# Attention and MLP on one Trainium2 core: other slots for the background weight conversion, GpSimd's operand split a slot later, v asked for sooner, one result of the mixing pairs later

## The chip, the core and the metric

The kernel runs on one core of a Trainium2 chip. The metric is the device time of one execution in microseconds. The engines in what follows are TensorE (PE, with its weight loads as PEld), VectorE (DVE), ScalarE (ACT), GpSimd (POOL) and SyncE (SP), which here does nothing but issue DMAs, in program order.

## The reference, cut to what matters

```python
scores = scale * np.matmul(q, k.transpose(0, 1, 3, 2))      # 4 batches, 8 heads, 576 x 576, head size 64
...
scores = scores + bias.transpose(2, 0, 1)[None, :, :, :]    # bias from a small net on log distances
attn = np.exp(scores - max) / (sum + 1e-09)
x = (attn @ v) laid out as 4 x 576 x 512
h = x.transpose(0, 2, 1) @ U @ V                             # mixing along the sequence, rank 32
u = x + h.transpose(0, 2, 1)
out = u + np.maximum(u @ w_ch1, 0.0) @ w_ch2                 # 512 -> 2048 -> 512
```

U, V, w_ch1 and w_ch2 arrive as 64-bit floats, seen as pairs of 32-bit words. The kernel turns them into 32-bit floats on the chip; that is the conversion the change is about.

## The kernel before

**Pairs and slots.** Two heads of one batch make a pair; there are 16 (p = 0 to 15, four to a batch). A pair has nine slots (s = 0 to 8), and `slot(p, s)` writes the instructions of one slot for all engines; each engine then runs its own list in that order. In a slot TensorE computes one block of scores (`sc`, L319). VectorE adds the bias and takes the row extreme (`p` or `praw`, L321), which is also what frees the scores' PSUM bank (two banks). ScalarE takes the exponential (L340). TensorE transposes earlier blocks (`tb`, `tm`, `ti`, L387 to L407), ScalarE or VectorE copy them to `pt`, and two runs of 20 matmuls multiply with v (`o`, L423): half 0 of a pair at the end of its slot 8, half 1 in slot 3 of the next pair. `assemble(p - 1, 0)` and `assemble(p - 1, 1)`, in slots 4 and 8, transpose that product (`tx`) and write it, scaled, to `x_sb` on VectorE (L446, L369). The transposes and `tx` share three PSUM banks in turn.

**The split.** Matmuls take q and k as a high part (`hi`) and a remainder (`lo`). GpSimd makes them for the next pair in four steps, `prep_ops`: high of q (L151), remainder of q (L159, two instructions), high of k (L151), remainder of k (L159, two), one step per slot from slot 2 on. They read `raw`, a single buffer that SP refills in two parts in slots 5 and 7 for the pair after next. `v` of the next pair is asked for in slot 7 and has two buffers. GpSimd also scales a block called `pm` in slot 1 (L360, two instructions).

**The conversion.** `conv_ops` gives the seven operations of one job of 128 x 256 values: a load of `wraw` (SP); size and low (ScalarE, L187 and L190); clamp, shift and join (VectorE, L193, L199, L205); add (GpSimd, L210). Twenty jobs run behind attention: one for U, three for V, sixteen for the first quarter of the weights. `pipeline` chops a job into the groups [size, low], [clamp, shift], [join, add]; `background(1)` issues one group after each slot in `conv_at` from `CONV_FROM` on. Once it is running, the odd job has its groups in slots 7, 8 and 0 and the even one in slots 1, 2 and 6.

**Mixing pairs.** After a batch is complete, pairs 5, 9 and 13 also run the mixing: `mix_t` in slot 0, then `mix_h` for rows 4, 0, 1, 2, 3 in slots 1 to 5. Each `mix_h` has VectorE add into `x_sb` (L485) and SP write that block of `x_sb` to `u_dram` (L486). `assemble(p - 1, 0)` of such a pair overwrites blocks 0, 1 and 4 of `x_sb`, which those writes must have read by then.

**After attention** the MLP runs on TensorE (L569, L592), with further conversions behind it.

Of the kernel before, what the change touches and what calls it, by code (L numbers as in the profile page):

```python
# [19 lines left out]
HP = H // 2  # L20
# [8 lines left out]
K0 = 2 * S + LEFT  # L29
QKW = 2 * K0  # L30
# [7 lines left out]

AV_NEW, AV_OLD, AV_LAST = 8, 3, 2

CONV_FROM = (2, 0)
F64_LO = 2.0**-15
F64_HI = (1.875 - 2.0**-23) * 2.0**16

# [2 lines left out]
def kernel(  # L47
# [82 lines left out]
    def load_part(p, a, e):  # L130
        b, hp = divmod(p, HP)
        for lo in (0, D):
            nc.sync.dma_start(out=raw[lo : lo + D, a:e], in_=qk[b, hp, :, a:e])

    def load_v(p):
        b, hp = divmod(p, HP)
        v_t[p] = vpp.tile([P, 640], F32, tag="v", name="v")
        nc.sync.dma_start(out=v_t[p], in_=vp[b, hp])
# [36 lines left out]
    def conv_ops(src, n, finish):  # L175
        st = {}

        def load():
            st["raw"] = wrawp.tile([P, CW], I64, tag="wraw", name="wraw")
            nc.sync.dma_start(out=st["raw"][:, 0:n], in_=src)  # L180
            words = st["raw"].bitcast(I32).rearrange("p (n t) -> p n t", t=2)
            st["l"], st["h"] = words[:, 0:n, 0], words[:, 0:n, 1]

        def size():
            st["t"] = wcp.tile([P, CW], I32, tag="t", name="wt")[:, 0:n]
            st["y"] = wyp.tile([P, CW], I32, tag="wy", name="wy")[:, 0:n]
            nc.scalar.activation(out=st["t"].bitcast(F32), in_=st["h"].bitcast(F32), func=AF.Abs)  # L187

        def low():
            nc.scalar.activation(out=st["y"], in_=st["l"].bitcast(U32), func=AF.Copy, scale=2.0**-29)  # L190

        def clamp():
            nc.vector.tensor_scalar(  # L193
                out=st["t"].bitcast(F32), in0=st["t"].bitcast(F32),
                scalar1=F64_LO, scalar2=F64_HI, op0=ALU.max, op1=ALU.min,
            )

        def shift():
            nc.vector.tensor_scalar(  # L199
                out=st["t"], in0=st["t"], scalar1=3, scalar2=0x3FFFFFF8,  # L200
                op0=ALU.logical_shift_left, op1=ALU.bitwise_and,
            )

        def join():
            nc.vector.scalar_tensor_tensor(  # L205
                out=st["t"], in0=st["h"], scalar=sgn, in1=st["t"], op0=ALU.bitwise_and, op1=ALU.bitwise_or
            )

        def add():
            nc.gpsimd.tensor_tensor(out=st["y"], in0=st["t"], in1=st["y"], op=ALU.add)  # L210

        return load, [size, low, clamp, shift, join, add], lambda: finish(st["y"].bitcast(F32))
# [77 lines left out]
    def new_pair(p):  # L290
        st = stp.tile([P, 32], F32, tag="st", name="st")
        pair[p] = {"st": st, "P": {}}
# [87 lines left out]
    def tr(p, c, hd, eng):  # L380
        hf, o = q_off(c)
        pt = get_pt(p, hf)
        src = pair[p]["P"][c]
        bank = psum("t", [P, 4, P], "tb")
        b0 = 0 if hd == 0 else S + LEFT
        for kb in range(4):
            nc.tensor.transpose(bank[:, kb, :], src[:, b0 + kb * P : b0 + (kb + 1) * P], ident)  # L387
        copy(eng, pt[:, 5 * hd : 5 * hd + 4, o : o + P], bank)
# [99 lines left out]
    NP = B * HP  # L488

    def slot(p, s):  # L490

        new, old = p < NP, p > 0
        if new:
            scores(p, s)
        if old and s == (AV_OLD if new else AV_LAST):
            av(p - 1, 1)
        if old and s == 0:
            tr(p - 1, 3, 0, "a")
        elif old and s == 1:
            tr(p - 1, 3, 1, "a")  # L500
            tr_mid(p - 1, 1, "d")
        elif old and s == 4:
            assemble(p - 1, 0)
        elif old and s == 8:
            assemble(p - 1, 1)
        if new and 3 <= s <= 8:
            c, hd = divmod(s - 3, 2)
            tr(p, c, hd, "a" if p % HP == 1 and 2 < s < 6 else "da"[hd])
            if s == 5:
                tr_m(p, "a")  # L510
            elif s == 6:
                tr_mid(p, 0, "d")
        if new:
            exps(p, s)
        if s > 0 and new:
            recip(p, s - 1)
        elif s == 0 and old:
            recip(p - 1, 8)
        if new and s == AV_NEW:
            av(p, 0)  # L520
# [15 lines left out]
    def load_acc(i):  # L536
        nc.sync.dma_start(out=acc[i], in_=u_dram[i * P : (i + 1) * P, :])
# [76 lines left out]
    def fin_w(dst):  # L614
        return lambda y: nc.sync.dma_start(out=dst, in_=y)

    def pipeline(jobs):


        ops = [conv_ops(*j) for j in jobs]  # L620
        groups = [[ops[0][0], ops[1][0]]]
        end = None
        for i, (_, o, fin) in enumerate(ops):
            if i + 2 < len(ops):
                groups[-1].append(ops[i + 2][0])
            size, low, clamp, shift, join, add = o
            groups += [[size, low], [clamp, shift], [join, add]]
            if end is not None:
                groups[-2].append(end)
            end = fin  # L630
        return groups + [[], [end]]

    def weight_jobs(g, fin):
        jobs = []
        for which in range(2):
            for k in range(KD):
                for a in range(0, DM, CW):
                    if which == 0:
                        src = w_ch1[k * P : (k + 1) * P, g * DM + a : g * DM + a + CW]
                    else:  # L640
                        r = (g * FG + k) * P
                        src = w_ch2[r : r + P, a : a + CW]
                    jobs.append((src, CW, fin(g, which, k, a, a + CW)))
        return jobs

    queue = []
# [54 lines left out]
    jobs = [(u32, 160, fin_u)]  # L701
    jobs += [(v4[:, a : min(a + CW, 640)], min(CW, 640 - a), fin_v(a, min(a + CW, 640))) for a in range(0, 640, CW)]
    jobs += weight_jobs(0, lambda g, which, k, a, e: fin_w(wq_dram[4 * which + k, :, a:e]))
    queue += pipeline(jobs)
    queue[1:1] = [[]] * 3

    conv_at = (0, 1, 2, 6, 7, 8)

    def big_views(t, parts):

# [20 lines left out]
    for p in range(NP):  # L731
        if p > 0:
            new_pair(p)
        if 0 < p < HP - 1:
            bias[p + 1] = big.tile([P, 9 * S], F32, tag=f"big{p + 1}", name=f"bias{p + 1}")
            loads = [o for c in (4, 0, 1, 2, 3) for o in bias_loads(c, p + 1)]
        for s in range(9):
            if s == (1 if p else 0) and p < NP - 1:
                prep = prep_ops(p + 1)
            if s in ((2, 3, 4, 5) if p else (0, 1, 2, 3)) and p < NP - 1:  # L740
                prep.pop(0)()
            if s in (5, 7) and 0 < p < NP - 2:
                load_part(p + 2, *((0, K0) if s == 5 else (K0, QKW)))
            if s == 7 and 0 < p < NP - 1:
                load_v(p + 1)
            for o in loads[0:2]:
                o()
            del loads[0:2]
            if p > 0 or s not in early.values():
                if p > HP and p % HP == 1 and s == 0:  # L750
                    mix_t(p // HP - 1)
                slot(p, s)
                background(int(s in conv_at and (p, s) >= CONV_FROM))
            if p > HP and p % HP == 1:
                for c in {1: (4,), 2: (0,), 3: (1,), 4: (2,), 5: (3,)}.get(s, ()):
                    mix_h(p // HP - 1, c)
            if p == NP - 3 and s == 1:
                t = big.tile([P, 9 * S], F32R, tag="big0", name="w1q")
                *wq[0], uth[0] = big_views(t, [(WQ, KD), (WQ, KD), (LINE, None), (UT, KD)])
                feed = first_weights(0)  # L760
            if p == NP - 2 and s == 1:
                t = big.tile([P, 9 * S], F32R, tag="big1", name="w2q")
                w2a, w2b, utl[0] = big_views(t, [(WQ, KD), (WQ, KD), (LINE, None), (UT, KD)])
                wq[0] += [w2a, w2b]
                feed = first_weights(1)
            if p == NP - 1 and s == 1:
                t = big.tile([P, 9 * S], F32, tag="big2", name="acc")
                acc.update(enumerate(big_views(t, [(DM, 0)] * 10)))
                feed = iter(())
            if p >= NP - 3 and s in (1, 2, 4, 5, 7, 8):  # L770
                next(feed, None)
            if p == NP - 1 and s in (1, 2, 3, 4, 5):
                load_acc(2 * s - 2)
                load_acc(2 * s - 1)
            if p == NP - 1 and s in (6, 7):
                make_ut(0, s - 6)
# [64 lines left out]
    for n in range(2, NG * NB + 1):  # L841
        g, j = divmod(n, NB)
# [88 lines left out]
```

## Time and profile before

| what | value |
|---|---|
| median of 3 runs (lowest, highest) | 767.35 us (767.05, 771.42) |
| the profiled execution's own time | 770.71 us |
| its span in the profile | 768.9 us |
| PE, DVE, ACT, POOL busy | 739.8, 442.5, 358.4, 237.9 us |
| mean granted TensorE clock | 0.997 of full speed |

The profile is one execution. Busy time of TensorE is modelled and says little about how long it waits; the waits are read from the idle time noted on a row, and from the chain of work that ended last. Pairs are told apart by the start of the matmuls with v in slot 8: pair 10, for example, lies between 232.97 and 250.38 us, and its slot 0 begins when that run of matmuls of pair 9 ends.

### The profile page before, as it was taken

Reading aid. Unit: us, or ns where it says so; the run is one execution under the profiler, and the core shown is the slowest. Engines: PE = TensorE matmul, PEld = TensorE weight load, DVE = VectorE, ACT = ScalarE, POOL = GpSimd, SP = SyncE. Lnnn points to the kernel's source line nnn. Section 1 sums busy time; section 2 is a strip of 40 time slices with the busy share of each in tenths; the row PEclk is TensorE's granted clock in tenths of the full one; section 3 lists DMA queues with packets and bytes.
Section 4 is the critical chain, followed back from the end, with each engine's and each line's share of the span. In section 5 each row is a group of like instructions: output and inputs, shape, how many; then the busy total and the mean of one; then the engine's idle time right before and its main releaser. Section 6 shows DMA issues by size and latency. Waiting matters only on the chain.

```text
span 768.9 us, 14017 instructions
## 1 busy us (share of the span) xinstructions
PE 739.8 (96%) x5380; PEld 616.7 (80%) x5380; DVE 442.5 (58%) x942; ACT 358.4 (47%) x803; POOL 237.9 (31%) x252
## 2 busy tenths in 40 slices
PE   6989998999999998999999999999999999999998
PEld 4436786777777777878889889988999999899986
DVE  7995588788878875752448734662237722221222
ACT  7996776777767775873125513431124410111010
POOL 0004658646655556620015502540015500000000
PEclk9999999999999999999999999999999999999999
DMA  7798995464445444540153301320002200001111
GB/s 213 244 313 271 260 267 148 135 177 131 125 144 165 137 120 135 155 140 1 35 192 110 97 1 42 98 81 1 1 28 83 69 1 1 1 28 55 55 42 68
DMA packets 41618, 84.02 MB, mean 109 GB/s; under 512 B 7248, under 2 KB 9936, under 8 KB 41296
## 3 DMA queue, kind: packets, MB, share of 16 engines
q1 hardware_dynamic: 41552, 83.13, 36.4%
q8 instruction: 42, 0.69, 0.4%
q14 instruction: 24, 0.20, 0.1%
HBM read 60.96 MB, written 22.15 MB: 108 GB/s over the span
## 4 chain that ended last, share of the span: by engine, by line
PE 70%; DVE 10%; ACT 8%; DMA 5%; issue 3%; POOL 2%; SPq 1%; DVEq 0%; ACTq 0%; POOLq 0%
PE po L592 24%; PE ph L569 23%; PE o L423 7%; PE sc L319 6%; PE tb L387 4%; ACT ring L244 2%; DVE p L321 2%; ACT p L340 2%; DVE wt L199 2%; DVE wt L193 2%; ACT ring L266 2%; DMA bias_dram<-ring 1%; DMA v<-in_vp_dram 1%; DMA raw<-in_qk_dram 1%; DVE wt L205 1%
## 5 line engine op out<-in xcount | busy, mean ns | idle before, releaser
L574 ACT ACTIVATE hh<-ph 128x1024 fp32r<-128x1024 f32 x36 | 36.9, 1026 | 207.5 <-PE ph L569 207.5
L575 DVE SCALAR_TENSOR_TENSOR hh<-ph,hh 128x1024 fp32r<-128x1024 f32 x36 | 44.1, 1224 | 141.4 <-ACT hh L574 141.4
L210 POOL TENSOR_TENSOR wy<-wt,wy 128x256 int32<-128x256 int32 (+1 forms) x68 | 50.0, 735 | 239.3 <-DVE wt L205 215.5
L340 ACT ACTIVATE p<-p,st 128x576 f32<-128x576 f32 x128 | 99.8, 780 | 30.6 <-DVE st L321 30.6
L319 PE MATMUL sc<-hi 128*128 128x288 f32 x320 | 100.9, 332 | 2.7 <-DVE st L321 2.7
L592 PE MATMUL po<-wq,hh 128*128 128x512 f32 x432 | 103.2, 395 | 0.0
L321 DVE CUSTOM_DVE_ANT_0 p<-sc,bias 128x576 f32<-128x576 f32 x128 | 95.5, 749 | 12.4 <-PE sc L319 7.1
L592 PE MATMUL po<-w2q,hh 128*128 128x512 f32 x432 | 101.7, 391 | 0.9 <-DVE acc L595 0.9
L592 PEld LDWEIGHTS po<-wq,hh 128*128 128x128 f32 x432 | 80.1, 188 | 17.5
L569 PE MATMUL ph<-ut,w1q 128*128 128x256 f32 x768 | 94.2, 280 | 0.0
L592 PEld LDWEIGHTS po<-w2q,hh 128*128 128x128 f32 x432 | 79.9, 188 | 17.1 <-issue 1.1
L569 PEld LDWEIGHTS ph<-ut,w1q 128*128 128x128 f32 x768 | 92.1, 188 | 1.5 <-issue 0.6
L595 DVE TENSOR_TENSOR acc<-po,acc 128x512 f32<-128x512 f32 x72 | 49.5, 689 | 73.2 <-PE po L592 73.2
L569 PEld LDWEIGHTS ph<-ut,wq 128*128 128x128 f32 x768 | 90.3, 188 | 1.4
L569 PE MATMUL ph<-ut,wq 128*128 128x256 f32 x768 | 90.6, 277 | 0.0
L319 PE MATMUL sc<-lo,hi 128*128 128x288 f32 x320 | 89.7, 296 | 0.3 <-POOL lo L159 0.3
L423 PE MATMUL o<-pt,v 128*64 128x320 f32 (+1 forms) x640 | 85.4, 411 | 2.9 <-DMA v<-in_vp_dram 2.8
L387 PE MATMUL tb<-ident,p 128*128 128x128 f32 x512 | 78.8, 277 | 5.1 <-DVE x_sb L369 3.2
L319 PEld LDWEIGHTS sc<-hi 128*128 128x128 f32 x320 | 60.6, 189 | 15.4 <-issue 6.6
L387 PEld LDWEIGHTS tb<-ident,p 128*128 128x128 f32 x512 | 60.2, 141 | 14.4 <-ACT p L340 7.3
L423 PEld LDWEIGHTS o<-pt,v 128*64 128x64 f32 x640 | 44.4, 137 | 33.0 <-DMA v<-in_vp_dram 3.1
L367 ACT COPY pt<-tb 128x512 f32<-128x512 f32 x88 | 50.9, 578 | 27.6 <-PE tb L387 27.6
(92 smaller groups left out, 1044.0 us busy)
## 6 DMA issues: line engine op xcount, KB each, us to landing
raw<-in_qk_dram SPq DMA_DIRECT2D x56, 304.0 KB, 4.6
wraw<-in_w_ch_dram SPq DMA_DIRECT2D x64, 256.0 KB, 2.7
bias_dram<-ring SPq DMA_DIRECT2D x36, 288.0 KB, 4.3
v<-in_vp_dram SPq DMA_DIRECT2D x16, 320.0 KB, 5.4
bias<-bias_dram SPq DMA_DIRECT2D x16, 288.0 KB, 5.7
acc<-u_dram SPq DMA_DIRECT2D x18, 256.0 KB, 4.8
out_dram<-acc SPq DMA_DIRECT2D x18, 256.0 KB, 2.0
bias<-bias_dram SPq DMA_DIRECT2D x16, 256.0 KB, 5.5
```

Of the source, the lines that this page charges most:

```text
L210: nc.gpsimd.tensor_tensor(out=st["y"], in0=st["t"], in1=st["y"], op=ALU.add)
L319: mm(ps[:, a, 0:HALF], lhsT=hi[:, q0 : q0 + P], rhs=kk, start=(i == 0), stop=(i == n - 1))
L321: nc.vector.tensor_tensor_reduce(out=halves(dst), in0=ps[:, :, 0:HALF], in1=halves(bias[hp][:, s * S : (s + 1) * S]), scale=-0.125, scalar ...
L340: nc.scalar.activation(out=dst, in_=dst, func=AF.Exp, bias=st[:, s : s + 1], scale=-1.0, accum_out=st[:, 10 + s : 11 + s])
L367: nc.scalar.copy(out=out, in_=in_)
L387: nc.tensor.transpose(bank[:, kb, :], src[:, b0 + kb * P : b0 + (kb + 1) * P], ident)
L423: mm(o[hd * D : (hd + 1) * D, 0:n], lhsT=v[:, vb * D : (vb + 1) * D], rhs=pt[:, pb, :], start=(j == 0), stop=(j == 4),)
L569: mm(st["ps"][:, f, :], lhsT=w, rhs=u[:, k, :], start=(i == 0), stop=(i == 3 * KD - 1))
L574: nc.scalar.activation(out=hh[n], in_=st["ps"], func=AF.Relu)
L575: nc.vector.scalar_tensor_tensor(out=hl[n], in0=st["ps"], scalar=0.0, in1=hh[n].bitcast(F32), op0=ALU.max, op1=ALU.subtract)
L592: mm(ps, lhsT=h, rhs=w, start=(m == 0), stop=(m == 3 * FG - 1))
L595: nc.vector.tensor_tensor(out=a, in0=ps, in1=a, op=ALU.add)
```

## The change

`by_twos` takes the place of `pipeline` for the conversions behind attention. It takes two jobs a and b at a time and makes five groups: [size a, low a, a load, the end of the job before], [size b, low b], [clamp a, shift a], [join a, add a], [clamp b, shift b, join b, add b, the end of a, a load]. With `conv_at = (0, 2, 6, 7, 8)` and a start in slot 6 of pair 2 these fall in slots 6, 7, 8, 0 and 2; slot 1 carries none. The split's steps move from slots 2 to 5 to slots 3 to 6, the loads of `raw` from slots 5 and 7 to 6 and 8, and the load of v from slot 7 to slot 4. In mixing pairs `assemble(p - 1, 0)` moves from slot 4 to slot 6.

```diff
-CONV_FROM = (2, 0)
+CONV_FROM = (2, 6)
...
-        elif old and s == 4:
+        elif old and s == (6 if p > HP and p % HP == 1 else 4):
             assemble(p - 1, 0)
...
+    def by_twos(jobs):
+
+        ops = [conv_ops(*j) for j in jobs]
+        for load, _, _ in ops[:2]:
+            load()
+        groups, end = [], None
+        for i in range(0, len(ops), 2):
+            (_, a, end_a), (_, b, end_b) = ops[i : i + 2]
+            ahead = [load for load, _, _ in ops[i + 2 : i + 4]]
+            groups += [
+                a[0:2] + ahead[0:1] + ([end] if end else []), b[0:2], a[2:4], a[4:6], b[2:6] + [end_a] + ahead[1:2]
+            ]
+            end = end_b
+        return groups + [[end]]
...
-    queue += pipeline(jobs)
-    queue[1:1] = [[]] * 3
-
-    conv_at = (0, 1, 2, 6, 7, 8)
+    conv_at = (0, 2, 6, 7, 8)
...
-            if s in ((2, 3, 4, 5) if p else (0, 1, 2, 3)) and p < NP - 1:
+            if s in ((3, 4, 5, 6) if p else (0, 1, 2, 3)) and p < NP - 1:
                 prep.pop(0)()
-            if s in (5, 7) and 0 < p < NP - 2:
-                load_part(p + 2, *((0, K0) if s == 5 else (K0, QKW)))
-            if s == 7 and 0 < p < NP - 1:
+            if s == 4 and 0 < p < NP - 1:
                 load_v(p + 1)
+            if s in (6, 8) and 0 < p < NP - 2:
+                load_part(p + 2, *((0, K0) if s == 6 else (K0, QKW)))
+            if (p, s) == (CONV_FROM[0], 0):
+                queue += by_twos(jobs)
```

What the engines' lists look like at three places. First GpSimd over one plain pair with conversions (`pm` in slot 1, `hi` and `lo` the split, `wy` the add of a job). Before:

```order
L360 TENSOR_SCALAR pm<-praw,st 128x576
L360 TENSOR_SCALAR pm<-praw,st 128x64
L151 TENSOR_SCALAR hi<-raw 128x1216
L159 TENSOR_TENSOR hi<-raw,hi 64x608 x2
L151 TENSOR_SCALAR hi<-raw 128x1216
L159 TENSOR_TENSOR lo<-raw,hi 128x608 x2
L210 TENSOR_TENSOR wy<-wt,wy 128x256 x2
```

After, the same stretch:

```order
L360 TENSOR_SCALAR pm<-praw,st 128x576
L360 TENSOR_SCALAR pm<-praw,st 128x64
L210 TENSOR_TENSOR wy<-wt,wy 128x256
L151 TENSOR_SCALAR hi<-raw 128x1216
L159 TENSOR_TENSOR hi<-raw,hi 64x608 x2
L151 TENSOR_SCALAR hi<-raw 128x1216
L159 TENSOR_TENSOR lo<-raw,hi 128x608 x2
L210 TENSOR_TENSOR wy<-wt,wy 128x256
```

One of the two adds, which waits for VectorE's join of slot 2, now stands ahead of the whole split.

On VectorE, slots 2 and 3 of the same kind of pair (`p` the scores, `wt` the job's intermediate). Before:

```order
L352 RECIPROCAL st<-st 128x1
L321 ISA p,st<-sc,bias_889 128x576
L321 ISA st 128x1
L193 TENSOR_SCALAR wt<-wt 128x256
L199 TENSOR_SCALAR wt<-wt 128x256
L321 ISA p,st<-sc,bias_889 128x576
L321 ISA st 128x1
L369 COPY pt<-tb 128x4x128
```

After:

```order
L352 RECIPROCAL st<-st 128x1
L321 ISA p,st<-sc,bias_889 128x576
L321 ISA st 128x1
L193 TENSOR_SCALAR wt<-wt 128x256
L199 TENSOR_SCALAR wt<-wt 128x256
L205 SCALAR_TENSOR_TENSOR wt<-wraw,sgn,wt 128x256
L321 ISA p,st<-sc,bias_889 128x576
L321 ISA st 128x1
L369 COPY pt<-tb 128x4x128
```

Clamp and shift stay where they were, the join comes up to them from slot 6; GpSimd's list beside them has changed.

On VectorE in a mixing pair, slots 3 to 6 (`mh` the mixed rows, `tx` the product of the pair before). Before:

```order
L485 TENSOR_TENSOR x_sb<-mh,x_sb 128x512
L321 ISA p,st<-sc,bias_106 128x576
L321 ISA st 128x1
L446 TENSOR_TENSOR x_sb<-tx,st 128x2x128
L369 COPY x_sb<-tx 64x128
L485 TENSOR_TENSOR x_sb<-mh,x_sb 128x512
```

After:

```order
L485 TENSOR_TENSOR x_sb<-mh,x_sb 128x512
L321 ISA p,st<-sc,bias_106 128x576
L321 ISA st 128x1
L446 TENSOR_TENSOR x_sb<-tx,st 128x2x128
L369 COPY x_sb<-tx 64x128
L369 COPY pt<-ti 128x256
```

The write to `x_sb` from `tx` now stands behind the last of the mixing's four additions of 128 rows instead of between the second and the third.

## Rows read from the trace of the kernel before

**Rows 1.** Windows, one per pair: us, busy time of each engine, PEclk, DMA.
```profile
158.87:176.09 17.22, 16.89 (x128) 13.09 (x130) 14.36 (x35) 12.87 (x33) 10.55 (x11) 1.00 0.56 153
...
232.97:250.38 17.41, 16.77 (x128) 13.11 (x130) 14.48 (x37) 12.89 (x33) 10.73 (x11) 1.00 0.53 147
```

**Rows 2.** Chain that ended last, pair 10: start us, us, what.
```profile
240.86 1.24 DVE wt L193
...
242.12 1.55 DVE wt L199
243.67 0.67 DVE p L321
...
250.38 2.84 PE o L423 x20
```

**Rows 3.** Timeline of PEld, pair 10: start us, us, instruction [idle before it <-releaser].
```profile
244.40 0.19 PEld L319 LDWEIGHTS sc<-hi 128*128 128x128 f32 x1 [0.44 <-DVE st L321]
...
245.30 0.42 PEld L387 LDWEIGHTS tb<-ident,p 128*128 128x128 f32 x4 [0.34 <-ACT p L340]
246.26 0.42 PEld L395 LDWEIGHTS tm<-ident,pm 128*128 128x128 f32 x4 [0.54 <-issue]
```

**Rows 4.** Timeline of POOL, pair 10.
```profile
239.73 1.04 POOL L360 TENSOR_SCALAR pm<-praw,st 128x576 f32<-128x576 f32 x2 [0.39 <-DVE st L352]
240.73 1.21 POOL L151 TENSOR_SCALAR hi<-raw 128x1216 fp32r<-128x1216 f32 x1
242.02 2.99 POOL L159 TENSOR_TENSOR hi<-raw,hi 64x608 fp32r<-64x608 f32 x2
...
246.40 2.96 POOL L159 TENSOR_TENSOR lo<-raw,hi 128x608 fp32r<-128x608 f32 x2
249.79 0.73 POOL L210 TENSOR_TENSOR wy<-wt,wy 128x256 int32<-128x256 int32 x1 [0.43 <-DVE wt L205]
```

**Rows 5.** Timeline of DVE, pair 3 and the end of pair 10.
```profile
116.29 1.58 DVE L205 SCALAR_TENSOR_TENSOR wt<-wraw,sgn,wt 128x256 int32<-128x256 int32 x1
...
251.97 0.28 DVE L193 TENSOR_SCALAR wt<-wt 128x256 f32<-128x256 f32 x1
...
254.63 0.76 DVE L321 CUSTOM_DVE_ANT_0 praw<-sc,bias 128x576 f32<-128x576 f32 x1 [2.05 <-PE sc L319]
...
255.43 0.43 DVE L205 SCALAR_TENSOR_TENSOR wt<-wraw,sgn,wt 128x256 int32<-128x256 int32 x1
```

**Rows 6.** Timeline of ACT, slot 7 of pair 10 to slot 0 of pair 11.
```profile
251.25 0.43 ACT L187 ACTIVATE wt<-wraw 128x256 f32<-128x256 f32 x1
...
254.96 0.59 ACT L367 COPY pt<-tb 128x512 f32<-128x512 f32 x1 [1.06 <-PE tb L387]
```

**Rows 7.** Timeline of PE in the mixing pairs 5, 9 and 13.
```profile
153.90 0.63 PE L395 MATMUL tm<-ident,pm 128*128 128x128 f32 x4 [0.77 <-ACT pt L367]
...
227.75 0.52 PE L387 MATMUL tb<-ident,p 128*128 128x128 f32 x3 [1.14 <-DVE x_sb L369]
...
302.76 0.41 PE L387 MATMUL tb<-ident,p 128*128 128x128 f32 x2 [2.05 <-DVE x_sb L369]
```

**Rows 8.** Chain that ended last, pair 13.
```profile
298.94 2.86 DMA u_dram<-x_sb
```

**Rows 9.** Windows in pair 13 and pair 3, columns as in Rows 1.
```profile
303.80:307.00 3.20, 3.20 (x14) 2.89 (x13) 1.54 (x5) 2.07 (x7) 2.95 (x3) 0.50 0.91 273
...
112.00:116.00 4.00, 4.00 (x36) 3.99 (x35) 3.97 (x12) 3.21 (x10) 2.86 (x3) 1.00 1.06 228
```

**Rows 10.** Timeline of PE, end of pair 3.
```profile
120.42 0.76 PE L423 MATMUL o<-pt,v 128*64 128x320 f32 x4 [2.82 <-DMA v<-in_vp_dram]
```

**Rows 11.** Timeline of POOL, end of pair 3: the split for pair 4.
```profile
118.76 1.21 POOL L151 TENSOR_SCALAR hi<-raw 128x1216 fp32r<-128x1216 f32 x1 [1.17 <-DMA raw<-in_qk_dram]
120.05 3.02 POOL L159 TENSOR_TENSOR lo<-raw,hi 128x608 fp32r<-128x608 f32 x2
```

## The prediction

> **What bounds the kernel now.** I read the windows by pair first: cut where the matmuls with v of slot 8 begin, a plain pair with conversions lasts 17.4 us [rows 1], and the six of them (6, 7, 8, 10, 11, 12) lie between 17.22 and 17.41. No engine is full there, so what matters is who keeps TensorE waiting. The chain of work that ended last says it: in the middle of pair 10 it leaves TensorE and runs through VectorE's clamp (1.24 us) and shift (1.55 us) of slot 2, and only then through the bias step of slot 3 at 243.67 [rows 2]. That step frees a scores bank and feeds ScalarE, and in TensorE's weight loads three waits follow: 0.44, 0.34 and 0.54 us [rows 3], 1.32 together. After the third, TensorE runs to the end of the pair without a wait of that size.
>
> Clamp and shift are slow only there. In slot 8, with nothing running on GpSimd, the clamp takes 0.28 us [rows 5]; for the shift, the same kind of instruction on as many values, I count 0.3. In slot 2 the clamp ends 0.15 us after GpSimd's first split step does (240.73 + 1.21 = 241.94 against 240.86 + 1.24 = 242.10), and the shift then lies in the shadow of the next one, which starts at 242.02 [rows 2, 4]. So some 2.2 us of VectorE go to standing behind GpSimd, once in every pair that converts.
>
> The mixing pairs have a second wait. VectorE's write of `tx` into `x_sb` has to wait until the write to `u_dram` has read its block; in pair 13 that DMA alone holds the chain for 2.86 us [rows 8]. TensorE, whose next transposes need the PSUM bank, waits 0.77, 1.14 and 2.05 us in pairs 5, 9 and 13 [rows 7]. In pair 13 the granted clock is then 0.50, the lower of the two levels (1.2 GHz), for at least 3.2 us [rows 9]; the long wait lies just ahead of it, and the plain pairs 6 and 10 stand at 1.00 [rows 1].
>
> Third, TensorE stands for 2.82 us at the end of pair 3 until v has landed [rows 10].
>
> **The change part by part.** *Slot 2, VectorE.* Size and low of job b now lie in slot 7 of the pair before, so the clamp waits for nothing of ScalarE's. GpSimd is then at `pm`, which ends at 240.77 at the latest (239.73 + 1.04) [rows 4], and behind `pm` stands the add of job b, which can't start before the join. So I let the clamp be held by all of `pm` and then count clamp 0.28, shift 0.3 and join 0.43 [rows 5]: VectorE is free at 241.8 at the latest, against 243.67 before [rows 2]. That is 1.9 us earlier, more than the 1.32 us that TensorE waits. The join also leaves slot 6, where it would have had its 0.43 us.
>
> By the Trainium skill, SBUF — State Buffer, section Who interferes with whom, a VectorE operation in a two-port mode and a GpSimd instruction share one port pair, whoever starts first keeps it for its whole instruction, and a VectorE operation with two inputs in SBUF is held too by a GpSimd instruction that reads there. The trace agrees: the join took 1.58 us beside the split in pair 3 and 0.43 us elsewhere [rows 5]. The rule speaks for the first part of this change and against the hope that it is over with it, since clamp and join can still meet `pm` and the late split; that is the first rival.
>
> I take 1.2 us of the 1.32 per pair (a few hundredths in each of the three rows are the gap that any such row has): **six pairs, 7.2 us.** The bounds are 0.6, if the later two waits stay in part, and 1.5.
>
> *Slot 2 to slot 0, GpSimd.* Here the change adds a wait: the add stands ahead of the split and waits for the join. From 241.8: add 0.73, high 1.21, remainder 2.99, high 1.21 again, remainder 2.96 [rows 4], with 0.1 us between them 9.5, so the split is done at 251.3. Queued behind the waiting add is nothing but the split; the one that waits for it is slot 0 of the next pair, whose first scores come 2.84 us after 250.38 [rows 2], 253.2 before, 251.9 if 1.32 us are gone. There the first half of `lo` is wanted (done at 249.8), the second some 0.3 us later. So 0.6 to 0.9 us are left: enough, but it was 3.8 before (246.40 + 2.96 = 249.4). I cost it at nothing; each microsecond beyond that cover would be one per pair.
>
> *Slot 8.* The clamp of job a came at 251.97, now at 250.7, while the split may run to 251.3. It can lose 0.6 us. Behind it VectorE idles 2.05 us until the next scores [rows 5], so this costs nothing either.
>
> *Slots 6 and 7, ScalarE.* Two activations of 0.43 us go from slot 1 to slot 6. ScalarE then has two jobs' activations back to back, and the exponentials of slots 7 and 8 come up to 0.9 us later; what needs them on TensorE lies behind the 2.84 us of matmuls with v, and ScalarE idles 1.06 us before its copy in slot 0 [rows 2, 6]. Nothing.
>
> *SP.* `raw` is asked for a slot later and a slot later wanted; the second part waits for the end of the split at 251.3 and is wanted only for the third split step of the next pair, over 10 us later. The loads of `wraw` and the writes of finished weights queue behind it on SP and are wanted five slots later at the soonest. Nothing in the plain pairs.
>
> *Mixing pairs.* In slot 6 the DMA of block 1 has two more slots to be read, over 3 us of matmuls; it took 2.86 [rows 8]. The bank's turn changes with the order, and the transposes behind need no other. So the three waits go, 0.77 + 1.14 + 2.05 = 4.0 us [rows 7], and with the 2.05 us, I expect, the low clock behind it: 3.2 us at half speed did the work of 1.6 [rows 9], so another 1.6. **Together 5.6 us.** Bounds: 2, if VectorE's additions and the contended clamp of slot 2 were the real hold in 5 and 9; 6.
>
> *v sooner.* It would give 2.8 us if nothing else were late. But `raw` for pair 4 landed at 118.76, and GpSimd finished its split at 120.05 + 3.02 = 123.07 [rows 11]; the scores of pair 4 began 2.9 us after 120.42 [rows 10], at 123.3. Without the wait for v they would be ready at 120.5 and stand for the split instead. And v now goes ahead of that part of `raw` in a stretch where the DMA engines are full (share 1.06 at 228 GB/s [rows 9]): 128 x 640 x 4 bytes are 1.4 us there. So the split ends near 124.5, the scores 0.4 us later than before. Bounds: +0.3 (raw not pushed back) to -1.4. Pair 4's own clamp is freed as in the others, which gives some 0.4 back. **Pairs 3 and 4 together: 0.**
>
> Sum: 7.2 + 5.6 + 0 = 12.8 us. Against its own execution that is 770.7 - 12.8 = 757.9 (the 1.8 us between span and time are the same in both). That execution lies 3.4 us above the median, and I can't tell whether the runs near 767 had the low clock of pair 13 too. With it 767.35 - 12.8 = 754.6, without it 756.2; I take 755.5.
>
> **The rivals.** *The collision moves instead of going.* The clamp meets `pm`, the join meets whatever GpSimd starts next, the clamp of slot 8 meets the end of the split. For it: all three are on GpSimd at those times. Against it: after `pm` GpSimd has nothing to start before the join, and slot 8 has cover. If half of the 1.2 us stays, the time is 755.5 + 3.6 = 759.
>
> *Only the mixing pairs gain*, because ScalarE, moved load and all, keeps the plain pairs where they are: 755.5 + 7.2 = 762.7. Against it: ScalarE is busy 12.89 of 17.41 us [rows 1], 80% of a pair of 16.2.
>
> *GpSimd's split becomes the bound, and the kernel gets slower.* Place: the add waiting for the join in slot 2 holds the whole split, and slot 0 waits for `lo`. It decides from the point where the join ends later than about 242.5. To lose everything that is won and 1% more, the split would have to come 2.5 us later than I have it, as when clamp, shift and join each paid a whole split instruction of 1.2 to 1.5 us; ten pairs by 2 us over the cover give 755.5 + 20 = 775. Nothing in GpSimd's list stands there to make them pay.
>
> *More than I count*: the upper bounds of the terms, 1.5 us for each plain pair, 6 for the mixing and 0.3 for v, give 15.3 us instead of 12.8, so 753.0.
>
> **How the numbers follow.** The forecast (754 to 758) gets 0.65, the moved collision (758 to 760.5) 0.14, mixing only (760.5 to 763.5) 0.10, more than counted (752.5 to 754) 0.06, the slower one 0.05. A measurement of this kernel tells about 1% from no change, so faster means below 759.7: 0.65 + 0.06 + two thirds of 0.14 = 0.80. Slower is 0.05, the rest 0.15. The range from 752.5 to 761 leaves out the slower case and most of the mixing only.
>
> **What would show it right or wrong.** Plain pairs of 16.1 to 16.3 us between the starts of the matmuls with v; clamp and shift of slot 2 with means near 0.3 us (the clamp up to 0.9 behind `pm`); TensorE's waits of 0.44, 0.34 and 0.54 gone; no wait of VectorE's `tx` write for `u_dram` in slot 6, and no stretch at clock 0.50 in pair 13; in pair 4 a wait of TensorE for `lo` in place of the one for v. The prediction is wrong if `lo` is waited for in every pair, if clamp and shift keep their 1.2 to 1.5 us, or if pair 3 really gets shorter without pair 4 getting longer.

## The result, and the profile after

The changed kernel takes **758.73 us** in the median (757.67 to 760.00) beside 767.20 (767.03 to 771.42) of the kernel before: a ratio of 0.988, 95% interval 0.984 to 0.992. In a second series on another chip it was 756.19 beside 767.61, ratio 0.985 (0.980 to 0.990). The forecast was 755.5, with 752.5 to 761.0 as its range.

The profiled executions stand at 770.71 and 757.67, 13.0 us apart, where the sum of the prediction was 12.8. The medians of the first series are only 8.5 apart, because the profile of before lay 3.5 us above its median and that of after 1.1 below. The ratios of the two series lie within each other's intervals, so the difference between their medians is not resolved. Where single executions differ, the runs below show in part.

Windows of the changed kernel: pairs 4, 5, 6, 10 and 13, a stretch in pair 4, and everything from pair 5 to slot 8 of pair 15; columns as in [rows 1].

```profile
117.28:137.43 20.15, 18.03 (x127) 14.73 (x127) 12.27 (x37) 13.44 (x36) 14.96 (x15) 0.92 0.57 144
137.43:158.21 20.78, 20.78 (x158) 16.17 (x157) 15.34 (x41) 15.11 (x38) 13.12 (x13) 1.00 0.51 150
158.21:174.30 16.09, 16.09 (x127) 13.10 (x126) 12.54 (x37) 12.65 (x34) 9.00 (x9) 1.00 0.65 165
227.25:243.32 16.07, 16.07 (x127) 13.10 (x126) 12.60 (x37) 12.70 (x34) 9.00 (x9) 1.00 0.63 166
275.49:296.35 20.86, 20.86 (x158) 16.20 (x157) 13.11 (x35) 14.31 (x35) 11.56 (x11) 1.00 0.58 172
124.00:128.00 4.00, 4.00 (x23) 3.98 (x21) 2.62 (x9) 3.00 (x7) 1.15 (x2) 0.57 0.83 216
137.43:331.46 194.03, 192.46 (x1488) 155.12 (x1487) 143.21 (x392) 148.37 (x371) 118.63 (x109) 1.00 0.55 151
```

Pair 6 went from 17.22 to 16.09 and pair 10 from 17.41 to 16.07 [rows 1], and TensorE's busy time (which is modelled) now fills both: no wait is left in its row, and in every trace below that has the two-job order the plain pairs last 16.05 to 16.10. The six plain pairs give 7.5 us together. Pairs 5, 9 and 13 went from 21.81, 22.09 and 24.57 to 20.78, 20.79 and 20.86, another 6.0; pair 13 runs at 1.00. Pairs 3 and 4 went from 35.41 to 36.09, a loss of 0.7, and pair 4 holds the only stretch at the lower clock (0.57 on average over 4 us; 3.41 us of them at 0.50).

VectorE in pair 10 of the changed kernel (the pair starts at 227.25), with slot 8 in the last two lines:

```profile
234.45 0.49 DVE L193 TENSOR_SCALAR wt<-wt 128x256 f32<-128x256 f32 x1
234.97 0.29 DVE L199 TENSOR_SCALAR wt<-wt 128x256 int32<-128x256 int32 x1
235.30 0.48 DVE L205 SCALAR_TENSOR_TENSOR wt<-wraw,sgn,wt 128x256 int32<-128x256 int32 x1
235.71 0.75 DVE L321 CUSTOM_DVE_ANT_0 p<-sc,bias 128x576 f32<-128x576 f32 x1
...
244.38 0.91 DVE L193 TENSOR_SCALAR wt<-wt 128x256 f32<-128x256 f32 x1
...
247.64 0.76 DVE L321 CUSTOM_DVE_ANT_0 praw<-sc,bias 128x576 f32<-128x576 f32 x1 [2.02 <-PE sc L319]
```

GpSimd beside it:

```profile
234.05 1.07 POOL L360 TENSOR_SCALAR pm<-praw,st 128x576 f32<-128x576 f32 x2 [0.38 <-DVE st L352]
235.87 0.73 POOL L210 TENSOR_TENSOR wy<-wt,wy 128x256 int32<-128x256 int32 x1 [0.75 <-DVE wt L205]
236.57 1.21 POOL L151 TENSOR_SCALAR hi<-raw 128x1216 fp32r<-128x1216 f32 x1
...
242.20 2.95 POOL L159 TENSOR_TENSOR lo<-raw,hi 128x608 fp32r<-128x608 f32 x2
```

The clamp of slot 2 went from 1.24 to 0.49 and the shift from 1.55 to 0.29 [rows 2]. The clamp runs beside the first of the two instructions of `pm`, which ends at 234.80 in the trace, and is done 0.14 us behind it; no split step lies beside it. The bias step of slot 3 comes 8.46 us into the pair instead of 10.62 (VectorE's own row in the two traces). The three waits of [rows 3] are gone. In slot 8 the clamp pays 0.91 behind the late split, and VectorE idles 2.02 us after that, as it idled 2.05 before [rows 5]: free of charge.

For the block that `assemble` writes, the view of line 446 lists what VectorE sat idle for. Before:

```profile
  DMA u_dram<-x_sb: 5.3, 5
  PE tb L387: 1.5, 1
  PE tx L443: 0.4, 1
```

After, the list has only the 0.4 us for `tx`; no write of it waits for `u_dram` any more. (The 1.5 us put down to `tb` are the write of pair 5, for which the run with the late write undone names `u_dram`, with 1.55 us.)

The price stands at the start of pair 4. TensorE there:

```profile
120.18 0.40 PE L319 MATMUL sc<-hi 128*128 128x288 f32 x1
121.76 0.40 PE L319 MATMUL sc<-lo,hi 128*128 128x288 f32 x1 [1.18 <-POOL lo L159]
...
123.22 0.40 PE L319 MATMUL sc<-lo,hi 128*128 128x288 f32 x1 [0.94 <-POOL lo L159]
...
124.67 0.44 PE L319 MATMUL sc<-lo,hi 128*128 128x288 f32 x1
```

and the chain that ended last, up to the same point:

```profile
109.87 8.87 DMA raw<-in_qk_dram
...
118.92 1.22 POOL hi L151
...
120.21 2.97 POOL lo L159 x2
```

The wait of 2.82 us for v [rows 10] is gone, and two waits for `lo` (1.18 and 0.94) stand in its place, 2.1 us, with 3.4 us at half clock behind them: a score matmul takes 0.44 us there and 0.29 to 0.30 elsewhere. `lo` is late because the second part of `raw` lands at 118.74; GpSimd's step behind it starts at 118.92, where it started at 118.76 before [rows 11].

### The profile page after: what moved, and what is told of

It is laid out like the page before. It is cut to its first block, busy times and chain, and to the rows that moved or that the text cites. A ratio compares the mean times of both kernels' runs of the same rounds, so it can differ in the third digit from the quotient of the medians.

```text
span 755.9 us, 14015 instructions
## 1 busy us (share of the span) xinstructions
PE 735.4 (97%) x5380; PEld 616.3 (82%) x5380; DVE 425.4 (56%) x942; ACT 357.9 (47%) x803; POOL 237.8 (31%) x252
## 4 chain that ended last, share of the span: by engine, by line
PE 77%; DMA 8%; ACT 6%; DVE 3%; issue 3%; POOL 1%; SPq 1%; ACTq 0%; POOLq 0%; DVEq 0%
PE po L592 24%; PE ph L569 24%; PE sc L319 9%; PE o L423 8%; PE tb L387 6%; DMA bias<-bias_dram 5%; ACT ring L244 2%; PE bs L255 1%; ACT ring L266 1%; DMA raw<-in_qk_dram 1%; DMA wraw<-in_w_ch_dram 1%; PE mt L463 1%; PE tx L441 1%; POOL wy L210 1%; ACT p L340 1%
```

## The experiments

My theory after the first comparison: plain pairs gain because clamp and shift no longer stand beside a split step, to which both the two-job order and the later split contribute; mixing pairs gain because the write no longer waits for `u_dram`; v sooner only swaps one wait for another. Where a time is compared with the kernel before, it is with runs of the same chip.

**v late again.**

```diff
-            if s == 4 and 0 < p < NP - 1:
+            if s == 7 and 0 < p < NP - 1:
                 load_v(p + 1)
```

> The changed kernel with v asked for in slot 7 again (all else stays). Theory: in the changed kernel v ahead of the second part of raw and of the weight loads only swaps one wait at the start of pair 4 for another: the 2.82 us for v are gone, but slot 0 waits 1.18 + 0.94 us for lo and a stretch of 3.4 us at granted clock 0.50 follows, so that pairs 3 and 4 last 36.09 us together against 35.41 before. With v late again I expect the wait of some 2.8 us for v at the end of pair 3, none for lo and no low clock in pair 4, both pairs together 34.5 to 35.4, and 757 to 759 in all beside 758.7. Rival: asking sooner is worth the wait that it removes, 2.8 us, and the low clock of pair 4 comes from elsewhere and stays: then 761.5.

Measured: 757.21 us (ratio 0.984, 0.979 to 0.989); pairs 3 and 4 together 35.07 us, clock 1.00 in both. The total and the sum of the two pairs came as the theory had them, the detail did not: TensorE waits for `lo` at the start of pair 3 (0.30 and 0.90 us) and of pair 4 (0.98), and, late as it is by then, not for v at all. So v sooner earned nothing here that v late lost. With v late this trace waits for `lo`, the run with two parts (below) for v: which transfer is late is not fixed by the slot of v alone.

**The late write undone.**

```diff
-        elif old and s == (6 if p > HP and p % HP == 1 else 4):
+        elif old and s == 4:
             assemble(p - 1, 0)
```

> The changed kernel with the first block of assemble in slot 4 of the mixing pairs again. Theory: the waits of TensorE of 0.8, 1.1 and 2.05 us in pairs 5, 9 and 13 belong to the write of tx that waits for the read of u_dram; they come back, and with the one of pair 13 the stretch at granted clock 0.50 behind it: 4.0 to 5.6 us, 762.7 to 764.3. Rival: in pairs 5 and 9 the real hold was VectorE's contended clamp and additions of slot 2, which the two-job layout has freed; then only pair 13 loses, 2 to 3.7 us: 760.7 to 762.4.

Measured: 761.90 us (ratio 0.991, 0.988 to 0.994). Pairs 5, 9 and 13 last 21.79, 22.16 and 22.16: 1.0, 1.4 and 1.3 us more, 3.7 together. The chain that ended last goes through the DMA again in pair 13:

```profile
290.86 2.01 DMA u_dram<-x_sb
...
293.06 0.42 DVE x_sb L446
293.49 0.20 DVE x_sb L369
...
293.82 0.63 PE tb L387 x4
```

So the waits of pairs 5 and 9 come and go with the place of this write too, against the rival. The total lies below the 762.7 that the theory allowed and in the rival's range, but because pair 13 kept granted clock 1.00 after its wait of 1.2 us; the low clock did not come back with the wait. For pair 5 it stays open how the write holds TensorE. The wait there is 0.77 us again, and the row names ScalarE's copy of `tb`, as in [rows 7]:

```profile
152.52 0.42 DVE L446 TENSOR_TENSOR x_sb<-tx,st 128x256 f32<-128x256 f32 x1 [1.55 <-DMA u_dram<-x_sb]
...
153.30 0.63 PE L395 MATMUL tm<-ident,pm 128*128 128x128 f32 x4 [0.77 <-ACT pt L367]
```

ScalarE's copy and VectorE's copy of `tx` end 0.02 us apart, and the edit moves the transposes into `tx` and their PSUM bank along with the write, so this run does not separate the two.

**The split early again.**

```diff
-            if s in ((3, 4, 5, 6) if p else (0, 1, 2, 3)) and p < NP - 1:
+            if s in ((2, 3, 4, 5) if p else (0, 1, 2, 3)) and p < NP - 1:
                 prep.pop(0)()
```

> The changed kernel with GpSimd's split in slots 2 to 5 again, conversions still by two jobs. GpSimd then has the first split step ahead of the add of job b. Theory: the plain pairs gain because clamp and shift of slot 2 no longer lie beside a split step; with the split back there, their means in the plain pairs go from 0.49 and 0.29 us to 0.9 or more for one of them, TensorE's waits behind the bias step come back, the six plain pairs last 16.8 to 17.4 instead of 16.1, and the total is 763 to 767. Rival: what helps is that size and low of job b are done a slot earlier, so that clamp and shift no longer wait in a chain; then the plain pairs stay within 0.2 us of 16.1 and the total at 758 to 760.

Measured: 757.17 us (ratio 0.985, 0.981 to 0.989), and the plain pairs at 16.05 to 16.10. My theory fell; the pairs are as the rival had them, and the total is even below its 758 to 760. VectorE in pair 10 of this run (the pair starts at 225.58):

```profile
232.78 0.49 DVE L193 TENSOR_SCALAR wt<-wt 128x256 f32<-128x256 f32 x1
233.31 0.29 DVE L199 TENSOR_SCALAR wt<-wt 128x256 int32<-128x256 int32 x1
233.64 1.30 DVE L205 SCALAR_TENSOR_TENSOR wt<-wraw,sgn,wt 128x256 int32<-128x256 int32 x1
234.86 0.74 DVE L321 CUSTOM_DVE_ANT_0 p<-sc,bias 128x576 f32<-128x576 f32 x1
```

and GpSimd:

```profile
232.38 1.07 POOL L360 TENSOR_SCALAR pm<-praw,st 128x576 f32<-128x576 f32 x2 [0.38 <-DVE st L352]
233.42 1.25 POOL L151 TENSOR_SCALAR hi<-raw 128x1216 fp32r<-128x1216 f32 x1
```

The split step is back directly behind `pm`, and clamp and shift are still short, because they begin as soon as the row step of slot 2 is done and are through before the split step holds anything. Only the join meets it, 1.30 us instead of 0.48. The bias step of slot 3 then comes 9.28 us into the pair, 0.8 later than in the changed kernel, and the pair is no longer for it: of the 2.2 us that the change frees on VectorE, TensorE needed at most 1.3. So what helps is not that GpSimd waits; by these rows it is that the clamp no longer waits for ScalarE. By the Trainium skill, SBUF — State Buffer, section Who interferes with whom, a VectorE operation with two inputs in SBUF is held by a GpSimd instruction that reads there. The join's 1.30 beside the split and 0.48 without agree.

**The later split alone**, in the kernel before.

```diff
-            if s in ((2, 3, 4, 5) if p else (0, 1, 2, 3)) and p < NP - 1:
+            if s in ((3, 4, 5, 6) if p else (0, 1, 2, 3)) and p < NP - 1:
                 prep.pop(0)()
```

> The kernel before with GpSimd's split a slot later, and nothing else of the change. Theory, after the run with the split early: what frees slots 2 and 3 in the plain pairs is the two-job order alone, because size and low of job b are done a slot earlier and the clamp no longer starts behind ScalarE's low. With the old order the clamp and the shift still start where GpSimd's first split steps do, the plain pairs keep 17.2 to 17.4 us, and the total stays within 2 us of before, 766 to 770. Rival: the later split takes part of the gain by itself, since GpSimd is then free while the clamp runs: plain pairs of 16.1 to 16.6 and 760 to 763.

Measured: 768.52 us beside 769.14, ratio 1.000 (0.997 to 1.002). Pair 10 lasts 17.42. VectorE there:

```profile
240.35 1.23 DVE L193 TENSOR_SCALAR wt<-wt 128x256 f32<-128x256 f32 x1 [0.65 <-ACT wt L187]
241.62 1.54 DVE L199 TENSOR_SCALAR wt<-wt 128x256 int32<-128x256 int32 x1
```

The clamp waits 0.65 us for ScalarE and then starts with the split step (240.23 to 241.44 on GpSimd), as in [rows 2, 4]. With nothing new ahead of it in GpSimd's list, a step that stands a slot later in the program starts at the same time. Together with the run before, the two-job order carries the whole gain of the plain pairs and the later split none of it. Within that order the part of the clamp's start is read from traces; no run moved size and low alone. Two other parts of it can be looked up. ScalarE has 0.9 us less to do in slot 1, but in pair 10 of the kernel before it stood waiting for VectorE's bias step just where TensorE's waits begin:

```profile
244.38 0.78 ACT L340 ACTIVATE p<-p,st 128x576 f32<-128x576 f32 x1 [1.65 <-DVE st L321]
```

and the join has left slot 6, where TensorE's row before notes no wait.

**The late write alone**, in the kernel before.

```diff
-        elif old and s == 4:
+        elif old and s == (6 if p > HP and p % HP == 1 else 4):
             assemble(p - 1, 0)
```

> The kernel before with the first block of assemble in slot 6 of the mixing pairs, and nothing else of the change. Theory: the hold on u_dram goes by itself, so pairs 5, 9 and 13 lose about the 1.0, 1.4 and 1.3 us that they got back when this part alone was undone, and pair 13 does not fall to granted clock 0.50: 3.7 us plus up to 2 of clock, 761.5 to 765.5. Rival: with the clamp and shift of slot 2 still contended VectorE is late in slot 6 as well, so the write meets the transposes behind it and less than half is gained: 766 to 768.

Measured: 763.84 us (ratio 0.993, 0.990 to 0.996). Pairs 5, 9 and 13 last 20.77, 20.80 and 20.85, as in the changed kernel. The stretches from pair 5 to slot 8 of pair 15 in this run, in the later split alone (with its pair 13), and in the late write undone:

```profile
138.87:340.45 201.58, 196.72 (x1489) 154.83 (x1488) 156.79 (x394) 149.14 (x373) 118.15 (x109) 1.00 0.53 148
```

```profile
136.55:342.17 205.62, 197.22 (x1489) 155.14 (x1488) 157.57 (x394) 149.36 (x373) 119.65 (x110) 1.00 0.52 145
284.40:307.01 22.61, 20.94 (x158) 16.23 (x157) 14.00 (x37) 14.90 (x35) 10.00 (x10) 1.00 0.53 147
```

```profile
136.37:334.12 197.75, 193.00 (x1489) 154.95 (x1488) 143.52 (x392) 148.44 (x371) 118.68 (x109) 1.00 0.53 149
```

The same stretch was 207.63 in the kernel before and is 194.03 in the changed one. That accounts for this stretch. From 205.62 to 201.58 the write gives 4.0 us; from 197.75 to 194.03, in the other order, 3.7. From 201.58 to 194.03 the two-job order gives 7.55. And 207.63 against 205.62 for kernels with the same work there is the low clock that pair 13 had in the profile of before (24.57 us) and not in the later split alone (22.61): 2.0 us, of which 0.4 is a shorter wait for the same write (1.67 us instead of 2.05) and 1.6 the clock.

**raw early again.**

```diff
-            if s in (6, 8) and 0 < p < NP - 2:
-                load_part(p + 2, *((0, K0) if s == 6 else (K0, QKW)))
+            if s in (5, 7) and 0 < p < NP - 2:
+                load_part(p + 2, *((0, K0) if s == 5 else (K0, QKW)))
```

> The changed kernel with raw asked for in slots 5 and 7 again, v still in slot 4. Theory: the low clock of pair 4 comes from TensorE's waits of 1.18 and 0.94 us for lo, which is late because the second part of raw lands at 118.74 us; asked for a slot (1.9 us) sooner it lands 1 to 2 us sooner, the waits shrink to less than 1 us, the clock stays at 1.00, and the total is 755.5 to 757.5. Rival: the DMA engines are full in that stretch, so what is asked for sooner lands no sooner or makes v or the bias late instead; then pairs 3 and 4 stay at 36 us and the total at 758.7.

Measured: 758.61 us (ratio 0.986, 0.982 to 0.991). The second part of `raw` was issued at 109.97 to 111.23, no sooner than the 109.36 to 109.87 of the changed kernel, GpSimd's step behind it started at 119.27, TensorE's waits were 1.18 and 0.93, and the low clock stayed. Asking a slot sooner did nothing here. By the chain that ended last the issue followed an earlier landing: of the first part of `raw` at 111.21 in this run, of a bias block at 109.29 in the changed kernel.

**v of pair 3 left out**, so that pair 3 multiplies with the v of pair 2.

```diff
         b, hp = divmod(p, HP)
+        if p == 3:
+            v_t[3] = v_t[2]
+            return
         v_t[p] = vpp.tile([P, 640], F32, tag="v", name="v")
```

> The changed kernel with the load of v for pair 3 left out, so that its last matmuls take the v of pair 2. Theory: with the DMA engines full, leaving out one transfer of 320 KB moves everything behind it ahead by its 1.0 to 1.4 us: the second part of raw for pair 4 lands at 117.4 to 117.8, the wait for lo in pair 4 shrinks by as much, and pairs 3 and 4 last 33.5 to 35 us instead of 36.09 (less if the low clock goes with it). Rival: the second part of raw is held by its own issue behind the split, not by what is ahead of it in the DMA engines; then it lands at 118.7 and nothing changes, 758.7.

Measured: 754.86 us (ratio 0.982, 0.978 to 0.986, which does not stand clear of the changed kernel's 0.980 to 0.990), and not by the mechanism expected. GpSimd, then TensorE (lines three further down in this kernel):

```profile
119.14 1.29 POOL L154 TENSOR_SCALAR hi<-raw 128x1216 fp32r<-128x1216 f32 x1 [1.52 <-DMA raw<-in_qk_dram]
```

```profile
122.06 0.40 PE L322 MATMUL sc<-lo,hi 128*128 128x288 f32 x1 [1.12 <-POOL lo L162]
...
123.53 0.40 PE L322 MATMUL sc<-lo,hi 128*128 128x288 f32 x1 [0.93 <-POOL lo L162]
```

`raw` landed at 118.96, no sooner without the 320 KB of v, and the waits for `lo` are those of the changed kernel within 0.06 us. So leaving v out did not bring `raw` forward. The rival was nearer in one thing: the chain reaches the second part of `raw` through GpSimd and the issue, not through another transfer's landing,

```profile
108.46 1.08 POOL pm L363 x2
109.54 0.11 SPq L133
...
109.69 9.27 DMA raw<-in_qk_dram
```

and in the changed kernel v of pair 3 was issued at 103.07 and took 4.2 us to land, so it was through before that part was issued at 109.87. Pair 4 was shorter (18.67 us instead of 20.15) because the clock stayed at 1.00 behind these waits.

**Two parts only:** the kernel before with the two-job order and the late write; split, raw and v stay in their old slots, so that against the changed kernel this is

```diff
-            if s in ((3, 4, 5, 6) if p else (0, 1, 2, 3)) and p < NP - 1:
+            if s in ((2, 3, 4, 5) if p else (0, 1, 2, 3)) and p < NP - 1:
...
-            if s == 4 and 0 < p < NP - 1:
+            if s in (5, 7) and 0 < p < NP - 2:
+                load_part(p + 2, *((0, K0) if s == 5 else (K0, QKW)))
+            if s == 7 and 0 < p < NP - 1:
                 load_v(p + 1)
-            if s in (6, 8) and 0 < p < NP - 2:
-                load_part(p + 2, *((0, K0) if s == 6 else (K0, QKW)))
```

> The kernel before with only the two-job order and the late write of the mixing pairs; split, raw and v stay where they were. Theory: these two parts carry the whole gain: plain pairs of 16.1, pairs 5, 9 and 13 of 20.8, pairs 3 and 4 between 32.5 and 36, and a total of 755 to 758.5. Rival: the later split and the sooner v each cover for the other in the run that undid only one of them; without both, v's 2.8 us come back on top of a wait for lo, and the total is 760 or more.

Measured, beside the changed kernel on one chip: 755.87 us (754.01 to 758.89) against 756.19 (753.23 to 762.19); ratio to before 0.984 (0.980 to 0.988). From pair 5 on it takes 194.02 us, the changed kernel 194.03. Its start shows the old wait in a trace:

```profile
122.27 2.91 PE L423 MATMUL o<-pt,v 128*64 128x320 f32 x20 [3.72 <-DMA v<-in_vp_dram]
```

With that wait, and none for `lo`, pairs 3 and 4 are 35.83 us. The two parts carry the whole gain, as far as these runs can tell.

**The changed kernel again**, unaltered.

> The changed kernel unaltered, beside the two others of this call on one chip. Theory: whether TensorE falls to granted clock 0.50 after the waits for lo in pair 4 differs from execution to execution, since equal waits (1.38 to 1.45 and 1.09 us) stood in four traces and the low clock behind them only in two; this profile then has the same waits with or without it, and the median is 757 to 760. Rival: the waits decide it; then pair 4 shows the low clock again and lasts 20.1 us.

Measured: 756.19 us (753.23 to 762.19), a little under the 757 to 760 expected. The profiled execution is the slowest of the six, 762.19. GpSimd there, and pair 4:

```profile
121.73 1.20 POOL L151 TENSOR_SCALAR hi<-raw 128x1216 fp32r<-128x1216 f32 x1 [1.26 <-DMA raw<-in_qk_dram]
```

```profile
118.80:141.16 22.36, 19.24 (x127) 15.81 (x126) 12.75 (x37) 14.21 (x38) 15.89 (x16) 0.85 0.56 138
141.16:335.21 194.05, 192.48 (x1488) 155.11 (x1487) 143.31 (x392) 148.28 (x371) 118.63 (x109) 1.00 0.54 152
```

Of the same program, `raw` lands some 2.8 us later than in the first profile, TensorE waits longer, the low clock follows, and pair 4 lasts 22.36 us. From pair 5 on the two executions differ by 0.02 us. The rival has this trace on its side and the waits are longer than the theory said, so this run does not tell the two apart; the traces of the other kernels do (last section). In TensorE's rows of those the waits stand at 1.12 to 1.18 and 0.93 or 0.94, not at the figures of the expectation.

**Another order of the transfers:** split in slots 2 to 5, raw in 5 and 7, v behind the second part of raw, and the third job's load behind that.

```diff
-                a[0:2] + ahead[0:1] + ([end] if end else []), b[0:2], a[2:4], a[4:6], b[2:6] + [end_a] + ahead[1:2]
+                a[0:2] + ahead[0 : i > 0] + ([end] if end else []),
...
+                b[2:6] + [end_a] + ahead[i > 0 : 2],
...
-            if s in ((3, 4, 5, 6) if p else (0, 1, 2, 3)) and p < NP - 1:
+            if s in ((2, 3, 4, 5) if p else (0, 1, 2, 3)) and p < NP - 1:
                 prep.pop(0)()
-            if s == 4 and 0 < p < NP - 1:
+            if s in (5, 7) and 0 < p < NP - 2:
+                load_part(p + 2, *((0, K0) if s == 5 else (K0, QKW)))
+            if s == 7 and 0 < p < NP - 1:
                 load_v(p + 1)
-            if s in (6, 8) and 0 < p < NP - 2:
-                load_part(p + 2, *((0, K0) if s == 6 else (K0, QKW)))
```

> The changed kernel with the split back in slots 2 to 5, raw in slots 5 and 7, v behind the second part of raw in slot 7, and the load of the third conversion job behind them too (two slots into pair 3). Theory: pairs 1 to 4 are paced by the DMA engines (share 1.0 from 80 to 120 us), whose transfers land in the order in which SP issues them; what can be won is that the second part of raw for pair 4 lands ahead of v (1.4 us) and of one weight load (1.1 us), so at 116 to 117.5 us instead of 118.74, with no low clock in pair 4. Pairs 3 and 4 together 32.5 to 34.5 us instead of 36.09, the rest as changed: 754 to 756.5. Rival: v then becomes the late one at the end of pair 3, by as much as is won for raw, and pairs 3 and 4 keep 35 us or more: 757 to 758.7.

Measured: 756.24 us (ratio 0.984, 0.980 to 0.988). GpSimd's step behind `raw` starts at 117.94 instead of 118.92; TensorE waits for no `lo` in pair 4, but for v before it:

```profile
118.91 2.91 PE L423 MATMUL o<-pt,v 128*64 128x320 f32 x20 [1.34 <-DMA v<-in_vp_dram]
```

Pairs 3 and 4 are 33.65 us, 2.4 under the changed kernel's. Once more, beside the changed kernel on one chip:

> The version with the split in slots 2 to 5, raw in 5 and 7 and v and the third job's load behind it, beside the changed kernel on the same chip. Theory: it has no wait for lo in pair 4 but some 1.3 us for v at the end of pair 3, so pairs 3 and 4 are 33.7 us, 2.4 under the changed kernel's: 1.5 to 3 us faster in the median. Rival: the order of the transfers only moves which of them is late; then the medians are within 1 us.

Measured: 755.17 us (753.90 to 756.92) beside 756.19 of the changed kernel; 1.0 us in the medians, which is less than the theory's 1.5 and than either interval resolves (0.978 to 0.987 against 0.980 to 0.990). Pairs 3 and 4 are 34.33 us. It has the lowest median of the three versions that ran side by side, by an amount that these runs don't secure. Its longest execution is 756.92 against 762.19, but that is one execution of six.

## Why the prediction was right

**The plain pairs** were priced at 7.2 us and gave 7.5. The step that named the cause holds in its first half: size and low of job b a slot earlier let the clamp start beside `pm`, ahead of the split, at 0.49 us instead of 1.24. The second half, that GpSimd then has nothing to start before the join, is true of the trace but not what the gain rests on (this answers the rival of the moved collision too); the run with the split early has a split step there beside the join and the same 16.07 us. I had reckoned VectorE free 1.9 us sooner against a need of 1.32; it was 2.16, and 1.3 were enough.

**The mixing pairs** were priced at 5.6 and gave 6.0: 1.03, 1.30 and 3.71 against 0.77, 1.14 and 3.65. The late write alone and its removal put 3.7 to 4.0 us on the place of the write, where the rows had 3.96. The reading of pair 5 was looser than I put it: its row names ScalarE's copy, not the write [rows 7], and the runs show there only that the wait comes and goes with the write's slot. The rest is the low clock of pair 13, 1.6 us as priced, which I took for a consequence of the wait. It stood in the profile of before, but neither in the later split alone, which keeps 1.67 us of the wait, nor in the run with the write undone, which has 1.2. So it was not shown to recur, and should not have stood whole in the sum (the forecast of 755.5 took it about half).

**The sum** was right to 0.2 us between the profiles, and part of that is luck: the terms were off by 0.3 and 0.4 us one way and by 0.7 the other, and 1.6 us of the gain is that clock. The forecast missed the first median by 3.2 us and the second by 0.7. The first lies where I had put the moved collision, 758 to 760.5, but the plain pairs at 16.05 to 16.10 rule that out. The single executions, 753.23 to 762.19 for the changed kernel on one chip, spread by more than the miss, and how many of them had a low clock the medians don't show.

**v sooner** was priced at nothing for the time and came to 0.7 us lost, by a working that was only half right; the loss of 0.7 lies inside the bounds I gave (+0.3 to -1.4). The wait for v did turn into one for `lo`. But I had v push `raw` back by 1.4 us and the split end near 124.5; `raw` landed where it did before and the split ended at 123.17. v had landed before the second part of `raw` was issued, and leaving v out altogether did not bring it forward. The loss comes from the low clock behind the two waits: from the end of `lo` to pair 5 it is 14.26 us in this trace, and 12.90 in the one with the write undone, which has the same waits at full clock; 1.4 us.

**The GpSimd term** at nothing held: the split of pair 10 ends at 245.15, the second score matmul of slot 0, which wants `lo`, starts at 246.40, and none of the six plain pairs waits for it. That leaves 1.2 us, against 0.6 to 0.9 reckoned. The rival that made GpSimd the bound decided from a join that ends 9.5 us into the pair (242.5 against 232.97); it ended at 8.5.

**What stays open** is what paces the landings between 80 and 120 us. The DMA share is about 1.0 there in every trace, yet the rate over 4 to 10 us ranges from some 215 to 335 GB/s, taking out 320 KB moved nothing, and the same program had `raw` 2.8 us apart in two executions. The order can be chosen; what a single transfer costs the others was not found.

## What to carry to other kernels

When an operation is slow beside another engine, ask first why it starts there: here it waited for a third engine, and the order that does that engine's work a slot earlier cured it, while moving the neighbour by a slot in the program moved nothing in time. Before pricing an edit at a stretch that is bound by transfers, see whether its wait stands in more than one execution; only what recurs belongs in the sum. And compare traces from a common event on: of the 4.5 us between the two executions of the changed kernel 3.7 lay ahead of pair 5 and 0.8 behind slot 8 of pair 15, and in between, where the clock stayed at 1.00, they agreed to 0.02 us, so that there the edits could be read.

## What the runs showed of the hardware

A wait of TensorE did not settle by its length whether the clock fell to the lower level (1.2 GHz) behind it. After two waits for `lo` of 1.18 and 0.93 or 0.94 us in pair 4, with the same work ahead of them, the granted clock fell in two traces (the changed kernel, and raw early) and stayed at 1.00 in two (the write undone with 1.18 and 0.93, and v left out with 1.12 and 0.93). After the 3.72 us for v in the run with two parts it stayed as well, but after 2.27 us for v in the run with the late write alone it fell, and the matmuls with v took 4.51 us instead of 2.91:

```profile
120.65 4.51 PE L423 MATMUL o<-pt,v 128*64 128x320 f32 x20 [2.27 <-DMA v<-in_vp_dram]
```

What decides it these traces do not show. Where it fell for 3.4 us it cost 1.4 to 1.6 us; in the changed kernel run again it was low for 6.83 us, and from the end of `lo` to pair 5 that execution took 15.2 us instead of 12.90, 2.3 more. So an edit that removes such a wait can gain that much more in one execution and not in another.
